# Turning q, k and x on TensorE in halves of 64 tokens instead of by DMA, and starting the row pairs two head pairs earlier

## The chip, the cores and the metric

The kernel runs on one core of one Trainium2 chip. The metric is the device time of one execution in microseconds. Three runs of the kernel before gave 306.70, 307.38 and 309.17 us, median 307.38. TensorE is called PE here, VectorE DVE, ScalarE ACT, GpSimd POOL, and SyncE SP.

## What is computed

Attention with a relative bias that depends on the distance of two tokens alone, and behind it a network of three gates, of which the largest counts:

```python
batch, n_heads, seq, head_dim = (8, 8, 576, 64)
...
scores = scale * np.matmul(q, k.transpose(0, 1, 3, 2))
...
scores = scores + bias.transpose(2, 0, 1)[None, :, :, :]
...
attn = np.exp(scores)
attn = attn / (np.sum(attn, axis=-1, keepdims=True) + 1e-09)
return np.matmul(attn, v).astype(np.float32)
...
h = np.maximum(np.maximum(x @ w1, x @ w2), x @ w3)
return (h @ w_out).astype(np.float32)
```

Inputs and output are float32. x is the attention's output as 4608 tokens of 512, the gates are 512 x 768, and `w_out` is 768 x 512.

## The kernel before

**Tiles.** The work is ordered by batch index (8) and, within it, by pair of heads (4): 32 pairs. Two heads of 64 fill the 128 partitions of `qT` and `kT`, which hold q and k with the head's dimension on the partitions and the tokens along the row. The 576 tokens are four tiles of 128 and a tail of 64. The tail's keys of both heads lie in one tile (`ktail`), head 0 in rows 0 to 63 and head 1 in rows 64 to 127.

**One pair.** PE makes the scores with keys on the partitions (`scores`, or `key_scores` where 512 queries of one key tile are made at once), ACT writes their exponentials to `e`, DVE multiplies the band near the diagonal by the exponentials of the bias (`times_band`). The tail's keys and queries go the same way (`left_keys`, `left_queries`, tile `el`). In the next pair PE multiplies `e` and `el` by the values and a column of ones (`attend`, `attend_rows`, tile `a`), and DVE divides by the sums and writes `x_sb` (`quotients`). The network needs x with the 512 features on the partitions, `xT`.

**The network beside it.** Its products are spread over the pairs in portions of 512 tokens. `ffn` makes a portion. From (2, 2) on, that is from batch index 2, pair 2, three pairs take two blocks of gates each and a fourth pair takes the outputs. What is left over waits in a list `pending`, out of which `fill` takes products.

**Row pairs.** From `ROWS = (3, 0)` on, every matmul works on 64 rows, two at a time on the two halves of the array, each with a PSUM bank of its own. `pair` (line 364) issues one half of such a product's matmuls, then with the halves swapped the other. In such a pair `run` of `gates` or of `outputs` fixes the order: first 8 matmuls of the first product, the third gate's largest value of the pair before on DVE, the fourth score tile, bands, the other 8 matmuls, ACT's copy, the second product, between them the left queries and the next pair's first score tile. The two pools for sums and for the network hold one tile of two banks each there, in place of two of one bank.

**PSUM.** All score tiles, `sc`, `sct` and `scq`, and the tiles `tp` in which q and k of batch index 1 are turned, take turns in the two buffers of one pool (`ps_s`, two banks a buffer). A tile that is given a buffer waits for the last reader of the tile before the last.

**Turning.** Batch index 0 is turned on PE (`first_transposes`, `more_transposes`, `x_transposes`). So is q and k of batch index 1 (`second_transposes`, line 781): ten transposes of 128 x 128 for a pair, q into one bank and k into the other, and two copies by DVE and two by ACT, declared independent as they read different banks. For batch indices 2 to 7 q and k are turned by DMA: `transposes` (line 724) puts 10 transposes for a batch index on SP's queue, and `turn_ahead` places them one batch index ahead. x of batch indices 1 to 7 is turned by DMA as well, five transposes for a batch index, from `quotients` of its last pair (lines 973 and 1021). SP also carries the early loads and the stores of the output.

**Loads.** POOL issues the loads. `begin_qk` loads half of a batch index's q and k two batch indices ahead; the rest and v follow one ahead. `in_turn` holds a load back until the loads some places before it have landed.

**Order.** PE, DVE and most of ACT keep the order of the program (`inorder`). From batch index 2, pair 2, on that holds for all exponentials; before, the exponentials may be moved by the scheduler.

Of the kernel before, what the change touches and what calls it, by code (L numbers as in the profile page):

```python
# [39 lines left out]
def kernel(  # L40
# [12 lines left out]
    nc = tc.nc  # L53
# [3 lines left out]
    P = 128  # L57
# [3 lines left out]
    QS = 2 * P  # L61
    QM = 2 * QS
    KT = 4
    ROWS = (3, 0)
    DEEP = 6
    PACKETS = 6 * QM
    FCH = d_ff // P
# [32 lines left out]
    def free_banks():  # L100
        ps_f.release()
        ps_a.release()
# [9 lines left out]
    def tr(*args):  # L112
        inorder(nc.tensor.transpose(*args))
# [14 lines left out]
    def other_banks(later, earlier):  # L128

        for a in later:  # L130
            for b in earlier:
                tc.declare_no_dep(a.ins, b.ins, reason="they read different PSUM banks")
# [588 lines left out]
            hook()  # L721


    def transposes(b):

        made = qk_tiles()
        qk.append(made)

        def pair(g):
            for j in range(2):  # L730
                inorder(nc.sync.dma_start_transpose(  # L731
                    out=made[j][:, g, 0 : KT * P].rearrange("p (t n) -> p t n", t=KT),
                    in_=batch[b][j][:, g].rearrange("p t h d -> p (t h d)"),
                ))

        def left():
            for j, n in enumerate((S - KT * P, P)):
                inorder(nc.sync.dma_start_transpose(  # L738
                    out=made[j][:, :, KT * P : KT * P + n],
                    in_=(qtail, ktail)[j][b % 2][0:n].rearrange("p h c -> p (h c)"),  # L740
                ))

        return [lambda: pair(0), left] + [lambda g=g: pair(g) for g in range(1, HP)]

    def qk_tiles():
        return [qkt.tile([P, HP, n], BF16, tag=x, name=x) for x, n in (("qT", S), ("kT", (KT + 1) * P))]

# [30 lines left out]
        tr(tp[:, QS : QS + P], qtail[0][:, hp, :], ident[:])  # L778
        dve_copy(qk[0][0][:, hp, QS:], tp[:, 0 : S - QS])

    def second_transposes(made, hp):

        hs = slice(2 * hp, 2 * hp + 2)
        tp = ps_s.tile([P, 2, 2 * CH], BF16, tag="sc", name="tp")
        for j, tl in enumerate((qtail, ktail)):
            for t in range(KT):
                tr(tp[:, j, P * t : P * t + P], batch[1][j][:, t, hs, :].rearrange("p h d -> p (h d)"), ident[:])
            tr(tp[:, j, KT * P : KT * P + P], tl[1][:, hp, :], ident[:])
        main = [
            copy(  # L790
                made[j][:, hp, 0 : KT * P].rearrange("c (p t) -> c p t", t=KT),
                tp[:, j, 0 : KT * P].rearrange("c (t p) -> c p t", t=KT),
            )
            for j, copy in enumerate((dve_copy, act_copy))
        ]
        tail = [
            copy(made[j][:, hp, KT * P :], tp[:, j, KT * P : n])
            for j, (copy, n) in enumerate(((dve_copy, S), (act_copy, (KT + 1) * P)))
        ]
        other_banks([main[1], tail[1]], [main[0], tail[0]])  # L800
        other_banks([tail[0]], [main[1]])

    def times_band(hp, e4, t, lo, hi, put=lambda x: x):
        lo, hi = max(lo, P * t - P), min(hi, P * t + 2 * P)
# [121 lines left out]
    def attend(b, hp, e4, el, half):  # L926

        x = ps_a.tile([P, 6, AW], F32, tag="a", name="a")
        v, vl = vx[b % 2], vt[b % 2]
        for i in range(2):
            t = 2 * half + i
            c = slice(P * t, P * t + P)
            mm(
                x[:, 2 * i : 2 * i + 2, :], lhsT=el[:, c], rhs=vl[:, hp, :, 0:AW],
                start=True, stop=False, skip_group_check=True,
            )
            for par in range(2):  # L940
                for kt in range(KT):
                    mm(
                        x[:, 2 * i + par, :], lhsT=e4[:, kt, par, c], rhs=v[:, kt, 2 * hp + par, 0:AW],
                        start=False, stop=(kt == KT - 1), skip_group_check=True,
                    )
        n = 2 + half
        if half:
            mm(
                x[:, 4:6, :], lhsT=el[:, S - P : S], rhs=vl[:, hp, :, 0:AW],
                start=True, stop=False, skip_group_check=True,  # L950
            )
            for par in range(2):
                for kt in range(KT):
                    mm(
                        x[:, 4 + par, :], lhsT=el[:, S - 64 + P * kt + 64 * par :][:, 0:P],
                        rhs=v[:, kt, 2 * hp + par, 0:AW],
                        start=False, stop=(kt == KT - 1), skip_group_check=True,
                    )

        def quotients():  # L960
            rd = nrm.tile([P, 6], F32, tag="rd", name="rd")
            inorder(nc.vector.reciprocal(rd[:, 0 : 2 * n], x[:, 0 : 2 * n, D]))
            divided[b, hp, half] = inorder(nc.vector.tensor_tensor(
                out=x_sb[b][:, 2 * half : 2 * half + n, P * hp : P * hp + P].rearrange("p t (h d) -> p t h d", d=D),
                in0=x[:, 0 : 2 * n, 0:D].rearrange("p (t h) d -> p t h d", h=2),
                in1=rd[:, 0 : 2 * n].rearrange("p (t h) -> p t h", h=2).unsqueeze(3).to_broadcast([P, n, 2, D]),
                op=ALU.mult,
            ))
            if b and hp == HP - 1:
                for t in range(2 * half, 2 * half + 2 + half):  # L970
                    c = b * S + P * t
                    w = min(P, S - P * t)
                    inorder(nc.sync.dma_start_transpose(out=xT[:, :, c : c + w], in_=x_sb[b][P - w :, t, :]))
        return quotients

    def attend_rows(b, hp, e4, el):
# [28 lines left out]
        def end():  # L1005
            behind_rows(rows(True)[0], last)

            def quotients():
                n = KT + 1
                rd = nrm.tile([P, 2, n], F32, tag="rd", name="rd")  # L1010
                a = x[:, :, 0 : n * AW].rearrange("p h (t d) -> p h t d", d=AW)
                inorder(nc.vector.reciprocal(rd[:], a[:, :, :, D]))
                inorder(nc.vector.tensor_tensor(
                    out=x_sb[b][:, 0:n, P * hp : P * hp + P].rearrange("p t (h d) -> p h t d", d=D),
                    in0=a[:, :, :, 0:D], in1=rd[:].unsqueeze(3).to_broadcast([P, 2, n, D]), op=ALU.mult,
                ))
                if hp == HP - 1:
                    for t in range(n):
                        c = b * S + P * t
                        w = min(P, S - P * t)  # L1020
                        inorder(nc.sync.dma_start_transpose(out=xT[:, :, c : c + w], in_=x_sb[b][P - w :, t, :]))
            return quotients
        return end

# [107 lines left out]
    for hp in range(HP):  # L1132
# [42 lines left out]
        else:  # L1175
# [11 lines left out]
            if hp == 2:  # L1187
                x_transposes(2, 0)
                x_transposes(3, 0)
            else:  # L1190
                begin_qk(2)
                x_transposes(0, 1)
                fill(8, lambda: second_transposes(qk[1], 0))
            products(hp, el)
        late.append(lambda hp=hp, e4=e4, el=el: attend(0, hp, e4, el, 1))

    turns = {n: [] for n in range(2, B)}
    places = {2: ((1, 1, 0), (1, 1, 1), (1, 2, 0), (1, 3, 1), (2, 1, 0)), 3: ((2, 2, 0), (2, 2, 1), (2, 3, 0), (3, 0, 0), (3, 0, 1))}
    for n in range(4, B):
        places[n] = tuple((n - 1, hp, half) for hp, half in ((1, 0), (1, 1), (2, 0), (2, 1), (3, 0)))  # L1200

    def turn_ahead(*place):

        for n, order in places.items():
            if place == order[0]:
                turns[n] = transposes(n)
            if place in order:
                turns[n].pop(0)()

    turned = [lambda hp=hp: x_transposes(hp, 1) for hp in range(1, HP)]  # L1210
    for b, hp in [(b, hp) for b in range(1, B) for hp in range(HP)]:
# [5 lines left out]
        tiled = bool(stages)  # L1217
        rows = (b, hp) >= ROWS
        if (b, hp) == ROWS:
            free_banks()  # L1220
            ps_a, ps_f = banks(1)
            pending.clear()
            thirds = [after]
        rate = 8 if b == 1 or (b, hp) == (2, 0) else 13


# [13 lines left out]
            for c, tt in order[:2]:  # L1240
                scores(qT, kT, e4, c, tt)
        store_outputs()
        turn_ahead(b, hp, 0)
        early()
        if turned:
            turned.pop(0)()
# [19 lines left out]
        if rows:  # L1266
# [19 lines left out]
            def ahead():  # L1286
# [3 lines left out]
                    key_scores(*(x[:, n % HP, :] for x in qk[n // HP]), begun[0][0], 0)  # L1290

            run(
                lambda: key_scores(qT, kT, e4, 3), left, ahead, largest, bands, lambda: left_keys_rows(qT, kT, el)
            )
            thirds.append(after)
        elif tiled:
# [35 lines left out]

            visit(qT, kT, e4, order[2:], None if together else beside_scores, el=el if together else None)
        store_outputs()
        turn_ahead(b, hp, 1)
        early()
        if turned:
            turned.pop(0)()
        if not together:
            quotients = next_late()  # L1340
            times_band(hp, e4, 1, 0, QM, inorder)
            quotients()
        if b == 1 and hp + 1 < HP:
            second_transposes(qk[1], hp + 1)
        if hp == 1 and b > 1:
            pending.extend((n, [fn]) for n, fn in rest)
            rest.clear()
# [1 line left out]
        if hp == 1 and b + 1 < B:  # L1349
# [81 lines left out]
```

## Time and profile before

| | |
|---|---|
| the runs' median | 307.38 us (306.70 to 309.17) |
| the profiled execution's own time | 306.96 us |
| its span, first to last instruction | 305.2 us |
| granted TensorE clock | 1.00 |
| PE busy from 72.05 to 96.63 us, pairs (2, 2) to (3, 0) | 23.99 of 24.58 us |
| PE busy from 96.63 to 245.85 us, pairs (3, 1) to (7, 3) | 148.96 of 149.22 us |
| PE busy from 245.85 us to the end | 55.58 of 59.35 us |
| transposes by DMA on SP's queue | 95 |

The span counts from the first to the last instruction of the program; the execution's own time has some 1.8 us more. A pair begins where PE starts on the sums of the pair before, `a<-vt,el`. Those starts are at 183.22, 191.01, 199.36 and 206.73 us: a pair with gates takes 7.79 us, the one with outputs 8.35, and the one behind it 7.37, since there a shorter product stands in the third gate's place. Matmuls overlap in the rows of the time line: a duration shown is that of the whole way through the array, and the work of a matmul is better read from the distance between two starts.

### The profile page before, as it was taken

The numbers are of one execution on the slowest core, as the hardware profiler recorded it, in microseconds if no ns is written. First come the engines' busy times: TensorE is split into PE (matmuls) and PEld (weight loads), VectorE is DVE, ScalarE is ACT, GpSimd is POOL, SyncE is SP. The second block draws the span as 40 slices with busy tenths as digits, with TensorE's granted clock in tenths as the row PEclk, the third lists the DMA queues.
The fourth block names the chain that finished last, engine by engine and source line by source line (L and its number), as shares of the span: only waits on it lengthen the run. The fifth ranks groups of instructions, "written<-read, shape, count | busy, mean of one in ns | idle before, by whom it ended". The sixth has DMA issues, their size and how long they took to land.

```text
span 305.2 us, 11001 instructions
## 1 busy us (share of the span) xinstructions
PE 295.5 (97%) x4745; PEld 183.7 (60%) x4745; DVE 206.3 (68%) x455; ACT 201.3 (66%) x270; POOL 143.7 (47%) x199
## 2 busy tenths in 40 slices
PE   8789999999999999999999999999999999999995
PEld 2367877765656676567666766676667654444442
DVE  6489888777776677676777677767776765453552
ACT  3999988977786787768776877677777720222211
POOL 8989677725839746774676469462000000000000
PEclk9999999999999999999999999999999999999999
DMA  9999999999999999999999999999623013202003
GB/s 160 187 203 194 176 137 120 114 165 128 223 150 121 150 131 205 174 143 192 181 139 135 202 162 146 138 197 171 79 46 140 6 40 94 84 0 108 31 0 137
DMA packets 165776, 40.51 MB, mean 133 GB/s; under 512 B 154584, under 2 KB 161248, under 8 KB 165728
## 3 DMA queue, kind: packets, MB, share of 16 engines
q0 software_dynamic: 105664, 16.66, 95.5%
q1 hardware_dynamic: 58304, 22.69, 41.6%
q8 instruction: 37, 0.61, 0.8%
q10 hardware_dynamic: 1760, 0.47, 0.7%
q14 instruction: 11, 0.09, 0.1%
HBM read 35.39 MB, written 9.45 MB: 147 GB/s over the span
## 4 chain that ended last, share of the span: by engine, by line
PE 80%; ACT 7%; DMA 6%; DVE 3%; SPq 2%; issue 1%; DVEq 0%; ACTq 0%
PE psp L109 32%; PE ps L109 15%; PE a L109 12%; PE sc L109 8%; PE pso L109 6%; ACT e L827 5%; DMA kT<-ktail 5%; PE sct L109 2%; PE warm L109 1%; PE scq L109 1%; ACT el L827 1%; SPq L738 1%; SPq L731 1%; DVE e L807 1%; DMA out_dram<-osb 1%
## 5 line engine op out<-in xcount | busy, mean ns | idle before, releaser
L827 ACT ACTIVATE e<-sc 128x1024 bf16<-128x1024 f32 x128 | 129.0, 1026 | 29.3 <-PE sc L109 28.0
L109 PEld LDWEIGHTS <-w_bf 64*128 64x128 bf16 (+1 forms) x1112 | 75.8, 95 | 55.3 <-issue 1.9
L109 PE MATMUL psp<-xT,w_bf 64*128 64x512 bf16 x784 | 97.2, 376 | 0.0
L807 DVE TENSOR_TENSOR e<-e,hank 128x512 bf16<-128x512 bf16 (+2 forms) x120 | 56.1, 473 | 13.9 <-ACT e L827 13.2
L109 PE MATMUL ps<-xT,w_bf 128*128 128x512 bf16 (+1 forms) x328 | 59.1, 332 | 0.0
L109 PE MATMUL sc<-qT,kT 64*128 64x256 bf16 (+1 forms) x352 | 48.5, 319 | 2.3 <-ACT e L827 1.1
L109 PEld LDWEIGHTS <-kT 64*128 64x128 bf16 (+1 forms) x712 | 30.0, 94 | 24.8 <-issue 6.8
L109 PE MATMUL a<-vx,e 64*128 64x65 bf16 (+1 forms) x1664 | 44.9, 190 | 0.0
L199 POOL DMA_DIRECT2D k_sb<-in_k_dram x48 | 36.2, 764 | 17.8 <-DMA vx<-in_v_dram 7.8
L199 POOL DMA_DIRECT2D q_sb<-in_q_dram x48 | 36.4, 767 | 15.1 <-DMA vx<-in_v_dram 5.7
L109 PEld LDWEIGHTS <-e 64*128 64x128 bf16 (+1 forms) x1664 | 40.8, 95 | 4.3
L109 PEld LDWEIGHTS <-hT 64*128 64x128 bf16 (+1 forms) x462 | 28.3, 95 | 18.7 <-DVE hT L551 1.6
L167 POOL DMA_DIRECT2D vx<-in_v_dram x28 | 24.8, 893 | 19.5 <-PE a L109 5.4
L109 PE MATMUL psp<-wo_bf,hT 64*128 64x256 bf16 (+1 forms) x360 | 31.7, 305 | 0.0
L421 ACT ACTIVATE m<-ps 128x512 bf16<-128x512 f32 x14 | 8.4, 597 | 34.3 <-PE ps L109 34.3
L827 ACT ACTIVATE el<-sct 128x576 bf16<-128x576 f32 (+2 forms) x36 | 21.7, 605 | 14.0 <-PE sct L109 13.9
L109 PEld LDWEIGHTS <-el 64*128 64x128 bf16 (+1 forms) x676 | 26.4, 94 | 7.0 <-issue 4.4
L109 PE MATMUL a<-vt,el 64*128 64x65 bf16 (+1 forms) x260 | 29.5, 198 | 0.2 <-DVE m L511 0.2
L551 DVE TENSOR_TENSOR hT<-psp,m 128x1024 bf16<-128x1024 f32 (+1 forms) x20 | 18.7, 956 | 9.1 <-PE psp L109 9.1
L109 PE MATMUL pso<-wo_bf,hT 128*128 128x512 bf16 (+2 forms) x102 | 21.7, 366 | 0.0
L430 DVE TENSOR_TENSOR m<-ps,m 128x512 bf16<-128x512 f32 x14 | 9.7, 692 | 17.0 <-PE ps L109 17.0
L537 DVE TENSOR_TENSOR m<-psp,m 128x1024 bf16<-128x1024 f32 x15 | 18.4, 1225 | 3.3 <-PE psp L109 3.1
(82 smaller groups left out, 292.8 us busy)
## 6 DMA issues: line engine op xcount, KB each, us to landing
out_dram<-osb SPq DMA_DIRECT2D x35, 256.0 KB, 4.7
vx<-in_v_dram POOLq DMA_DIRECT2D x28, 128.0 KB, 6.7
q_sb<-in_q_dram POOLq DMA_DIRECT2D x50, 64.0 KB, 5.3
k_sb<-in_k_dram POOLq DMA_DIRECT2D x48, 64.0 KB, 5.3
w_bf<-in_moe_w_dram POOLq DMA_DIRECT2D x2, 512.0 KB, 8.5
xT<-in_k_dram SPq DMA_DIRECT2D x6, 128.0 KB, 4.5
hank<-w_dr SPq DMA_DIRECT2D x2, 384.0 KB, 5.7
w_bf<-in_moe_w_dram POOLq DMA_DIRECT2D x1, 768.0 KB, 8.1
```

Source lines behind the costliest of these rows:

```text
L109: made = inorder(nc.tensor.matmul(*args, **kw))
L167: in_turn(b, nc.gpsimd.dma_start(out=dst[:, t, h0:h1, :], in_=x[:, t, h0:h1, :]), P * (h1 - h0))
L199: in_turn(b, nc.gpsimd.dma_start(out=dst[:, g, :, par, :], in_=part), KT * P)
L421: nc.scalar.activation(out=st[fb]["m0"][:], in_=ps0, func=ACTF.Copy)
L430: inorder(nc.vector.tensor_tensor(out=m[:], in0=ps1, in1=st[fb]["m0"][:], op=ALU.max))
L537: return lambda: inorder(nc.vector.tensor_tensor(out=m[0][:], in0=ps1(), in1=m[0][:], op=ALU.max,))
L551: inorder(nc.vector.tensor_tensor(out=out_[:, i : i + n], in0=ps2()[:, i : i + n], in1=m[0][:, i : i + n], op=ALU.max,))
L731: inorder(nc.sync.dma_start_transpose(out=made[j][:, g, 0 : KT * P].rearrange("p (t n) -> p t n", t=KT), in_=batch[b][j][:, g].rearrange(" ...
L738: inorder(nc.sync.dma_start_transpose(out=made[j][:, :, KT * P : KT * P + n], in_=(qtail, ktail)[j][b % 2][0:n].rearrange("p h c -> p (h c)"),
L807: put(nc.vector.tensor_tensor(out=e4[:, t, :, lo:hi], in0=e4[:, t, :, lo:hi], in1=hank[:, 2 * hp : 2 * hp + 2, c0:c1][:, :, ::-1], op=ALU. ...
L827: made = nc.scalar.activation(out=out_, in_=in_, func=ACTF.Exp, scale=inv_sqrt_d)
```

## The change

The transposes by DMA are gone, and with them `transposes`, `second_transposes` and the order by places. A function `turn(n)` is called once in each pair n (32 pairs, n = 4 b + hp), from pair 3 on and once behind the last. It turns on PE q and k of pair n + 1 and x of pair n - 1 (q and k up to batch index 7, x from batch index 1), each block of 128 tokens as two halves: 64 tokens on 64 rows, whose transpose of 128 x 64 goes to one bank of `tp` for the upper half and to the other for the lower. Tails are single halves or, for k, one pair. All lie in one tile of the pool of the scores. Every copy out of `tp` takes both halves, so it reads both banks: DVE copies q, q's tail and x, ACT copies k and x's tail. The declarations of independence are gone. A copy of batch index 1's q and k scatters the tokens, as before; from batch index 2 on the runs are 64 long.

Where it stands: in a row pair ahead of the fourth score tile, inside `run`; before the row pairs at the end of the pair, ahead of the last products and of the next pair's scores. Row pairs begin at (2, 2), and what is pending is drained ahead of them. `begin_qk` follows pair 2, not 1.

```diff
-    ROWS = (3, 0)
+    ROWS = (2, 2)
...
-    def second_transposes(made, hp):
+    def turn(n):
         tp = ps_s.tile([P, 2, 2 * CH], BF16, tag="sc", name="tp")
+        W = KT * 64
+        K, X = W + 64, 2 * W + 128
+        def half(h, c, src):
+            r = slice(64 * h, 64 * h + 64)
+            tr(tp[:, h, c : c + 64], src[r], ident[r, r])
+        def halves(c, src):
+            for h in range(2):
+                half(h, c, src)
...
+        b, hp = divmod(n + 1, HP)
+        new = b < B
+        if new:
...
+            for j, c in enumerate((0, K)):
+                for t in range(KT):
+                    part = batch[b][j][:, hp, t] if b > 1 else batch[b][j][:, t, 2 * hp : 2 * hp + 2]
+                    halves(c + 64 * t, part.rearrange("p h d -> p (h d)"))
+            halves(K + W, ktail[b % 2][:, hp, :])
+            half(0, W, qtail[b % 2][:, hp, :])
...
+        b_x, hp_x = divmod(n - 1, HP)
+        if b_x:
+            x = x_sb[b_x][:, :, P * hp_x : P * hp_x + P]
+            half(1, X + W, x[:, KT])
             for t in range(KT):
+                halves(X + 64 * t, x[:, t])
+        if new:
+            if b > 1:
+                dve_copy(by_half(q_to[:, 0 : KT * P], KT), turned(0, KT))
+                act_copy(by_half(k_to, KT + 1), turned(K, KT + 1))
+            else:
...
+            dve_copy(q_to[:, KT * P : S], tp[:, 0, W : W + 64])
+        if b_x:
+            to = xT[:, hp_x, b_x * S : b_x * S + S]
+            dve_copy(by_half(to[:, 0 : KT * P], KT), turned(X, KT))
+            act_copy(to[:, KT * P :], tp[:, 1, X + W : X + W + 64])
...
-        other_banks([main[1], tail[1]], [main[0], tail[0]])
-        other_banks([tail[0]], [main[1]])
...
         if (b, hp) == ROWS:
+            while pending:
+                fill(13)
             free_banks()
             ps_a, ps_f = banks(1)
             pending.clear()
-            thirds = [after]
+            thirds = [lambda: (lambda: None, lambda parts=1: lambda: None)]
...
-        turn_ahead(b, hp, 0)
...
             run(
-                lambda: key_scores(qT, kT, e4, 3), left, ahead, largest, bands, lambda: left_keys_rows(qT, kT, el)
+                lambda: (turn(HP * b + hp), key_scores(qT, kT, e4, 3)), left, ahead, largest, bands,
+                lambda: left_keys_rows(qT, kT, el),
             )
...
-        turn_ahead(b, hp, 1)
...
-        if b == 1 and hp + 1 < HP:
-            second_transposes(qk[1], hp + 1)
+        if not rows:
+            turn(HP * b + hp)
...
-        if hp == (2 if b == 1 else 1) and b + 2 < B:
+        if hp == 2 and b + 2 < B:
             begin_qk(b + 2)
...
     for put in [next_late() for _ in late[:]]:
         put()
+    turn(HP * B)
     fill(13)
```

More of the change, by code (lines that the diff above doesn't have):

```diff
@@ L721, in fill @@
             hook()
[L724 to L743, printed above, removed]
     def qk_tiles():
@@ L779, in more_transposes, with by_half, turned @@
         dve_copy(qk[0][0][:, hp, QS:], tp[:, 0 : S - QS])
-    def second_transposes(made, hp):
-        hs = slice(2 * hp, 2 * hp + 2)
+    def turn(n):
         tp = ps_s.tile([P, 2, 2 * CH], BF16, tag="sc", name="tp")
-        for j, tl in enumerate((qtail, ktail)):
-            for t in range(KT):
[L787 to L799, printed above, removed]
-        other_banks([main[1], tail[1]], [main[0], tail[0]])
-        other_banks([tail[0]], [main[1]])
+        W = KT * 64
[6 more added lines that the diff above has]
+                half(h, c, src)
+        def by_half(x, n):
+            return x.rearrange("c (t h n) -> c t h n", h=2, t=n)
+        def turned(c, n):
+            return tp[:, :, c : c + 64 * n].rearrange("c h (t n) -> c t h n", t=n)
+        b, hp = divmod(n + 1, HP)
+        new = b < B
+        if new:
+            if len(qk) == b:
+                qk.append(qk_tiles())
+            for j, c in enumerate((0, K)):
[4 more added lines that the diff above has]
+            half(0, W, qtail[b % 2][:, hp, :])
+            q_to, k_to = (x[:, hp, :] for x in qk[b])
+        b_x, hp_x = divmod(n - 1, HP)
+        if b_x:
+            x = x_sb[b_x][:, :, P * hp_x : P * hp_x + P]
+            half(1, X + W, x[:, KT])
+            for t in range(KT):
+                halves(X + 64 * t, x[:, t])
[4 more added lines that the diff above has]
+            else:
+                for copy, to, c in ((dve_copy, q_to, 0), (act_copy, k_to, K)):
+                    copy(to[:, 0 : KT * P].rearrange("c (h n t) -> c t h n", h=2, t=KT), turned(c, KT))
+                act_copy(by_half(k_to[:, KT * P :], 1), turned(K + W, 1))
+            dve_copy(q_to[:, KT * P : S], tp[:, 0, W : W + 64])
[3 more added lines that the diff above has]
+            act_copy(to[:, KT * P :], tp[:, 1, X + W : X + W + 64])
@@ L968, in quotients @@
             ))
[L969 to L973, printed above, removed]
         return quotients
@@ L1016, in quotients @@
                 ))
[L1017 to L1021, printed above, removed]
             return quotients
@@ L1192 @@
                 x_transposes(0, 1)
-                fill(8, lambda: second_transposes(qk[1], 0))
+                fill(8, lambda: turn(HP - 1))
             products(hp, el)
         late.append(lambda hp=hp, e4=e4, el=el: attend(0, hp, e4, el, 1))
[L1197 to L1208, printed above, removed]
     turned = [lambda hp=hp: x_transposes(hp, 1) for hp in range(1, HP)]
```

## The prediction, made before the result was known

> **What bounds the kernel now.** I read the page first, then the time line of one pair of heads in the middle, then the groups with their shapes kept apart, then the waits and the chain. A "pair" is one turn of the main loop, one pair of heads of one batch index; (3, 0) is batch index 3, pair 0.
>
> ```profile
> PE 295.5 (97%) x4745; PEld 183.7 (60%) x4745; DVE 206.3 (68%) x455; ACT 201.3 (66%) x270; POOL 143.7 (47%) x199
> ...
> PE 80%; ACT 7%; DMA 6%; DVE 3%; SPq 2%; issue 1%; DVEq 0%; ACTq 0%
> ```
>
> TensorE is the bound. The time line of pair (6, 0), from the first `a<-vt,el` at 183.22 to the next at 191.01, shows it without a hole (7.79 us; "PE psp x16" are two blocks of 0.86):
>
> ```profile
> 187.21 1.23 DVE L551 TENSOR_TENSOR hT<-psp,m 128x1024 bf16<-128x1024 f32 x1 [0.60 <-PE psp L109]
> ...
> 187.86 0.39 PE L109 MATMUL sc<-qT,kT 64*128 64x512 bf16 x2
> ...
> 188.09 1.90 PE L109 MATMUL psp<-xT,w_bf 64*128 64x512 bf16 x16
> 188.29 1.03 ACT L827 ACTIVATE e<-sc 128x1024 bf16<-128x1024 f32 x1 [0.53 <-PE sc L109]
> ...
> 189.21 1.02 ACT L123 ACTIVATE m<-psp 128x1024 bf16<-128x1024 f32 x1
> ...
> 189.81 0.30 PE L109 MATMUL scq<-qT,kT 64*128 64x64 bf16 x8
> 189.93 0.40 PE L109 MATMUL sc<-qT,kT 64*128 64x512 bf16 x2
> ...
> 190.15 1.04 PE L109 MATMUL psp<-xT,w_bf 64*128 64x512 bf16 x8
> ...
> 191.01 0.21 PE L109 MATMUL a<-vt,el 64*128 64x65 bf16 x2
> ```
>
> The new copies are priced from these groups:
>
> ```profile
> L827 ACT ACTIVATE e<-sc 128x1024 bf16<-128x1024 f32 x128 | 129.0, 1026 | 29.3 <-PE sc L109 28.0 <-issue 1.0
> ...
> L126 DVE COPY qT<-tp 128x512 bf16<-128x512 bf16 x4 | 2.7, 684 | 0.5 <-PE tp L113 0.5
> L123 ACT ACTIVATE kT<-tp 128x512 bf16<-128x512 bf16 x4 | 2.5, 624 | 0.0
> ...
> L123 ACT ACTIVATE kT<-tp 128x128 bf16<-128x128 bf16 x4 | 1.2, 312 | 0.0
> ...
> L126 DVE COPY kT<-tp 128x640 bf16<-128x640 bf16 x2 | 1.0, 481 | 0.0
> ...
> L126 DVE COPY kT<-tp 128x512 bf16<-128x512 bf16 x2 | 0.8, 420 | 0.0
> ...
> L126 DVE COPY qT<-tp 128x64 bf16<-128x64 bf16 x4 | 0.7, 181 | 0.0
> ```
>
> What the DMA transposes cost today is in the chain and in the waits:
>
> ```profile
> 82.17 8.31 DMA kT<-ktail
> ```
> ```profile
> PEld L109 <- DMA kT<-ktail: 0.8, 2, 0.5
> ```
>
> The chain gives one wait 8.31 us, but PE was busy for all of it but the last half microsecond. The waits say 0.8 us; the gaps between matmul starts are 0.51 us at 90.53 and 0.42 at 122.18. That is all there is to win: 0.9 us.
>
> **What goes.** 95 transposes leave SP's queue (q 24, k 24, tails 12, x 35); SP keeps loads and stores. Worth 0.9 us. Rows from (2, 2): in a row pair the sums' five tail products of 130 columns become pairs of 65 (0.13 us), and the left keys' 576 columns pairs of 288 (0.12). 0.25 us twice is 0.5; it is inside the pair times below. POOL's eleven loads of `begin_qk` go one pair later; their first reader is then five pairs (40 us) off and they land in about 5.3 us, so nothing. If that cover were gone, a late load would cost up to those 5.3 us.
>
> **What PE gets.** 28 turns of 19 halves (q, k) and 28 of 9 (x), 784 matmuls of 64 columns. Eight such ones, `scq`, take 0.12 us (189.81 to 189.93), 15 ns each: 12.1 us. Forty whole transposes at 56 ns go: net 9.8 us. In a pair: 0.43 us.
>
> **What stands behind it.** In a row pair the turn stands after the first 8 `psp` matmuls of the gate, ahead of the fourth score tile. Its tile `tp` takes one of the two buffers in which all score tiles go round. I read the waits of the built changed program: the copies out of `tp` wait for one another, since each reads both banks. DVE q (512), then ACT k (640), then DVE q tail (64), DVE x (512), then ACT x (64). Behind ACT's last one stand, in its queue, the exponentials of the fourth score tile, the gate's copy, the left queries and the next pair's first scores. PE's `scq` waits for the last copy (same buffer), PE's next `sc` for the exponentials of the fourth tile.
>
> Prices: q 0.42, as the 512-element copy in unbroken runs (the 684 ns one scatters its output; that is the upper bound); k by ACT's two rows, 312 + (640-128)/384 x 312 = 728 ns; q tail 0.18; x 0.42; x's rest 0.26 (same line). A hand-over between engines is 0.035 us in this trace, PE to a reader about 0.2 after the last issue. Chain: 0.42+0.73+0.18+0.42+0.26 and four hand-overs = 2.14 us.
>
> The Trainium skill, "PSUM — Partial Sum Buffer", section "PSUM bank collisions raise a hardware error", says two engines must not read one bank at once, so such readers are ordered. The old `second_transposes` kept its engines to one bank each, and the trace has them side by side:
>
> ```profile
> 44.20 0.78 DVE L126 COPY qT<-tp 128x512 bf16<-128x512 bf16 x2
> 44.27 0.80 ACT L123 ACTIVATE kT<-tp 128x512 bf16<-128x512 bf16 x2
> ```
>
> By that row alone the copies would take 1.05 us, by the rule 2.14; the waits of the program decide for 2.14.
>
> **A gate pair, step by step** (0 is its first `a<-vt,el`). PE reaches the turn at 4.64 today. Once the pair before ends late, 0.12 is added at the sums (they wait for `el<-el,hank`) and 0.2 at the third gate (its bank is freed by DVE's `m`): 4.95. Then the turn 0.43 and 0.2 to DVE: 5.58 (DVE's `hT` is done at 5.52). Copies: 7.72. Exponentials: 8.75. Next `sc` at 8.79, 0.22, last 8 `psp` 0.86: the pair ends at 9.87, and the next begins in the same state. Against 7.79: +2.08. Meanwhile PE has only 2.06 us (`sc` 0.22, `psp` 0.86 twice, `scq` 0.12) to hide 3.4.
>
> An output pair (8.35 today, (6, 1)): turn at 5.08, copies done at 7.87, and PE, which has 0.65 us to do after the turn, waits 1.75 for `scq`; then 2.9 us of its outputs and the scores, end 10.9. The pair after it (7.37 today): turn at 4.21, then 0.63 to DVE's start, 2.14 of copies, 1.07 of exponentials and hand-over, 1.08 of scores and `psp`: 9.15.
>
> Sum from 72.05 to 245.85 (173.8 us today): (2, 2) 10.7 (1.3 of waiting outputs, drained ahead of it; then, with no third gate of a pair before, the turn at 4.5, + 4.92 as above), (2, 3) and (3, 0) 9.87 each; five output pairs 54.5; five after them 45.75; eight gate pairs 79.0; (7, 3), which turns x alone, 8.1. Together 217.8: +44.0.
>
> **Before the rows** seven turns stand ahead of the next pair's scores. Those wait for k; the second score tile takes `tp`'s buffer and, with x in the turn, ACT puts the exponentials of the first tile ahead of x's rest. At 43.30: `x_sb` is done at 44.29, q (scattered) 44.97, k 45.95 (0.62 and, for its tail, 0.31), q tail 46.16, x 46.61, exponentials 47.1, x's rest 47.4: the second tile at 47.4, not 45.9, less 0.1 on PE: 1.4. At 50.50 less work covers it: 2.2. The turns ahead of (2, 0) and (2, 1), new ones with 0.87 us of cover: 2.5 each. The first two have no x: 0.9 and 0.35. The last has 2.6 us of outputs as cover: 0.5. Sum 10.4; bounds 5 (PE alone and half the waits) and 14 (every turn 2).
>
> **At the end** PE waits for the last `x_sb` (248.42, where it goes on at 247.35 today), then 9 halves: 1.2 us.
>
> Sum against the profiled execution's own 306.96 (span 305.2; 0.42 under the median of the three runs): 306.96 + 44.0 + 10.4 + 1.2 = 362.6. The median may lie 0.4 off that; I say 362. PE's 9.8 us are in it.
>
> Bounds: without the 0.3 in each pair and with 5 ahead of the rows, 306.96 + 38 + 5 + 1 = 351; with q and x at 684 ns, 0.52 in each of 21 turns, 373. Own range of this case: 350 to 375.
>
> **Rivals.**
> *Not slower: the DMA wait was real.* If the 8.31 and the 6.87 us that the chain gives `kT<-ktail` held PE, 15.2 go and 9.8 come, with the copies hidden: 301.6. It decides from 9.8 us of true waiting on; the gaps show 0.9. Chance 0.02.
> *PE's own work alone.* Copies hidden: 306.96 + 9.8 + 1.2 - 0.9 - 0.5 = 316.6. For it: ACT is busy 66%, DVE 68%. Against: the buffer is wanted 2.06 us after the turn. 0.04.
> *The copies run side by side* (1.05 in place of 2.14): 21 x 1.09 and 5 ahead of the rows less: 335. Against: the waits in the program. 0.07.
> *Copies at the slow rate, or the halves not two abreast* (0.43 more each): 373 to 375. For it: no row has runs of 64 that hop between two banks. 0.13.
> *The forecast:* 0.74.
>
> **How the numbers follow.** Time 362, of the likeliest. The range leaves out the first three rivals (0.13) and the edges: 344 to 377. One per cent is about what a measurement of this kernel can tell from none. Faster 0.02 (the first rival), within 1% 0.01, slower 0.97.
>
> **What would show it.** Gate pairs of 9.9 us, output pairs of 10.9; in each, ACT's `kT<-tp` right behind DVE's `qT<-tp` and DVE's tail copy behind that; PE waiting for ACT `xT` ahead of `scq` and for ACT `e` ahead of `sc`; PE's share down from 97% to about 86%; 64-column transposes at 15 ns. It is wrong if `scq` and `sc` start without a wait, if the q copy is not 0.42, or if the first turns cost nothing.

## The result and the profile after

The kernel after takes 364.69 us (median of 4 runs, 362.63 to 366.80), the kernel before 307.04 (4 runs, 306.62 to 309.17): a ratio of 1.186, 95% interval 1.177 to 1.195. The profiled execution took 362.63 us, its span is 360.9. The page of the kernel after has, against the lines shown of before:

```profile
PE 316.8 (88%) x5567; PEld 197.9 (55%) x5575; DVE 228.9 (63%) x524; ACT 223.9 (62%) x320; POOL 143.3 (40%) x199
...
PE 66%; ACT 18%; DVE 12%; issue 2%; DMA 1%; ACTq 0%
PE psp L109 22%; PE ps L109 13%; PE a L109 11%; ACT e L836 9%; PE sc L109 7%; ACT kT L123 6%; DVE qT L126 5%; PE pso L109 5%; PE tp L113 3%; DVE xT L126 2%; PE sct L109 2%; ACT xT L123 1%; PE warm L109 1%; DVE x_sb L972 1%; ACT el L836 1%
```

PE's share falls from 97% to 88%, though it is busy 21 us longer. The chain was on PE for 80% and is for 66%; ACT and DVE come in with the copies `kT`, `qT`, `xT` and with the exponentials `e` behind them.

The waits of the kernel after (us in total, times, longest) name the same links:

```profile
ACT kT L123 <- DVE qT L126: 30.2, 28, 1.8
DVE qT L126 <- ACT kT L123: 24.4, 28, 1.5
ACT xT L123 <- DVE xT L126: 18.1, 25, 3.5
...
PE sc L109 <- ACT e L836: 14.8, 23, 1.2
...
PE scq L109 <- ACT xT L123: 7.2, 6, 1.4
```

The time line of a gate pair of the kernel after, from its first `a<-vt,el` at 225.57 us to the next at 234.86, shows where the time goes. It answers to the pair from 183.22 to 191.01 of before.

```profile
230.22 0.30 PE L113 MATMUL tp<-ident,q_sb 64*128 64x64 bf16 x8
...
230.62 0.40 PE L109 MATMUL sc<-qT,kT 64*128 64x512 bf16 x2
...
230.84 0.42 DVE L126 COPY qT<-tp 128x512 bf16<-128x512 bf16 x1
231.30 0.70 ACT L123 ACTIVATE kT<-tp 128x640 bf16<-128x640 bf16 x1 [1.19 <-DVE qT L126]
...
232.04 0.19 DVE L126 COPY qT<-tp 128x64 bf16<-128x64 bf16 x1 [0.77 <-ACT kT L123]
232.15 0.41 DVE L126 COPY xT<-tp 128x512 bf16<-128x512 bf16 x1
...
232.59 0.22 ACT L123 ACTIVATE xT<-tp 128x64 bf16<-128x64 bf16 x1 [0.59 <-DVE xT L126]
232.71 1.02 ACT L836 ACTIVATE e<-sc 128x1024 bf16<-128x1024 f32 x1
232.87 0.29 PE L109 MATMUL scq<-qT,kT 64*128 64x64 bf16 x8
...
233.78 0.39 PE L109 MATMUL sc<-qT,kT 64*128 64x512 bf16 x2 [0.62 <-ACT e L836]
```

Read it downward: the bracket of a copy names the copy ahead of it, on the other engine. The fourth score tile is done at 231.02, but ACT, which must make its exponentials, stands in the row of copies until 232.71. Of these 1.69 us ACT spends 0.82 on its own two copies and waits 0.87 for DVE's. Counted by starts, PE loses time twice. Its 16 products from 230.84 on are issued by 232.56 (0.86 us for 8), but `scq` starts at 232.87, 0.06 us behind the last copy. And the next `sc` starts 0.91 us after `scq`, where it took 0.12 in the kernel before, because it waits for the exponentials. These 0.3 and 0.8 us are all that the pair takes beyond PE's own pace, which e1 below puts at 8.18 us. In an output pair PE has less to do meanwhile and stands longer, for the last copy. The time line of PE in the one from 234.86 to 245.33 us has:

```profile
242.32 0.29 PE L109 MATMUL scq<-qT,kT 64*128 64x64 bf16 x8 [1.42 <-ACT xT L123]
```

**Where the 55.7 us of span are.** The span splits at the first sums of (2, 2) and at the last pair's `a<-vt,el` (93.71 and 300.04 us after; 72.05 and 245.85 before):

| stretch | before | after | more | predicted |
|---|---|---|---|---|
| ahead of the rows | 72.05 | 93.71 | 21.7 | 11.7 (10.4 and 1.3 of drain) |
| row pairs | 173.8 | 206.3 | 32.5 | 42.7 (44.0 less that drain) |
| end | 59.35 | 60.86 | 1.5 | 1.2 |

The sum came out (55.6 predicted) because two errors of about 10 us cancel; that is luck. The experiments must explain both, not only the total.

### The profile page after: what moved, and what is told of

Read it like the earlier page. It is cut to its first block, busy times and chain, and to the rows that moved or that the text cites. A ratio compares the mean times of both kernels' runs of the same rounds, so it can differ in the third digit from the quotient of the medians.

```text
span 360.9 us, 12575 instructions
## 1 busy us (share of the span) xinstructions
PE 316.8 (88%) x5567; PEld 197.9 (55%) x5575; DVE 228.9 (63%) x524; ACT 223.9 (62%) x320; POOL 143.3 (40%) x199
## 4 chain that ended last, share of the span: by engine, by line
PE 66%; ACT 18%; DVE 12%; issue 2%; DMA 1%; ACTq 0%
PE psp L109 22%; PE ps L109 13%; PE a L109 11%; ACT e L836 9%; PE sc L109 7%; ACT kT L123 6%; DVE qT L126 5%; PE pso L109 5%; PE tp L113 3%; DVE xT L126 2%; PE sct L109 2%; ACT xT L123 1%; PE warm L109 1%; DVE x_sb L972 1%; ACT el L836 1%
## 5 line engine op out<-in xcount | busy, mean ns | idle before, releaser
L109 PE MATMUL psp<-xT,w_bf 64*128 64x512 bf16 x800 | 99.2, 376 | 0.6 <-DVE x_sb L1017 0.6
L109 PE MATMUL sc<-qT,kT 64*128 64x512 bf16 (+1 forms) x336 | 49.7, 329 | 22.2 <-ACT e L836 14.8
L816 DVE TENSOR_TENSOR e<-e,hank 128x512 bf16<-128x512 bf16 (+2 forms) x120 | 56.1, 472 | 14.6 <-ACT e L836 14.4
L109 PEld LDWEIGHTS <-kT 64*128 64x128 bf16 (+1 forms) x700 | 30.5, 94 | 57.1 <-issue 37.4
L126 DVE COPY qT<-tp 128x512 bf16<-128x512 bf16 (+3 forms) x63 | 22.9, 363 | 38.3 <-ACT kT L123 24.4
L109 PE MATMUL a<-vx,e 64*128 64x65 bf16 (+1 forms) x1728 | 45.7, 191 | 0.0
L109 PEld LDWEIGHTS <-e 64*128 64x128 bf16 (+1 forms) x1728 | 41.6, 95 | 4.2
L123 ACT ACTIVATE kT<-tp 128x640 bf16<-128x640 bf16 (+2 forms) x32 | 22.5, 735 | 30.2 <-DVE qT L126 30.2
L109 PEld LDWEIGHTS <-hT 64*128 64x128 bf16 (+1 forms) x462 | 29.5, 95 | 16.0 <-DVE hT L436 0.4
L109 PEld LDWEIGHTS <-el 64*128 64x128 bf16 (+1 forms) x702 | 27.5, 95 | 6.1 <-issue 3.5
L551 DVE TENSOR_TENSOR hT<-psp,m 128x1024 bf16<-128x1024 f32 (+1 forms) x21 | 19.9, 968 | 8.2 <-PE psp L109 8.2
```

What stands on the lines that cost most here:

```text
L109: made = inorder(nc.tensor.matmul(*args, **kw))
L123: return inorder(nc.scalar.activation(out=out_, in_=in_, func=ACTF.Copy))
L126: return inorder(nc.vector.tensor_copy(out_, in_))
L551: inorder(nc.vector.tensor_tensor(out=out_[:, i : i + n], in0=ps2()[:, i : i + n], in1=m[0][:, i : i + n], op=ALU.max,))
L816: put(nc.vector.tensor_tensor(out=e4[:, t, :, lo:hi], in0=e4[:, t, :, lo:hi], in1=hank[:, 2 * hp : 2 * hp + 2, c0:c1][:, :, ::-1], op=ALU. ...
```

## The experiments

The theory is that of the prediction: the copies out of `tp` hand over between DVE and ACT one after the other, ACT's queue stands behind them, and PE waits for what stands in that queue. Its rivals: PE's own transposes cost the time; the amount of copying costs it, whoever copies; the row pairs from (2, 2) on cost it. Ratios are to runs of the kernel before on the same chip, with 95% intervals. It took 306.8 to 307.7 us (medians) on these chips and 307.04 beside the kernel after, so differences in us to the kernel after may be off by some 1 us.

**e1, the transposes alone.** The kernel before, with the halves turned on PE as in the kernel after, from batch index 2 on for q and k, and nobody reading them; the DMA transposes stay.

```diff
+    def turn(n):      # as in the kernel after, the matmuls alone
...
-                lambda: key_scores(qT, kT, e4, 3), left, ahead, largest, bands, lambda: left_keys_rows(qT, kT, el)
+                lambda: (turn(HP * b + hp), key_scores(qT, kT, e4, 3)), left, ahead, largest, bands,
+                lambda: left_keys_rows(qT, kT, el),
...
+        if not rows and HP * b + hp > HP:
+            turn(HP * b + hp)
...
-        if hp == (2 if b == 1 else 1) and b + 2 < B:
+        if hp == 2 and b + 2 < B:
...
+    turn(HP * B)
```

> The kernel before, with the new 64-row transposes added where the changed kernel has them (q and k from batch index 2 on, x), but into a tile that nobody copies: the DMA transposes still do the work, and the transposes' own result is not used. This leaves PE's part of the change alone. Theory A (the copies out of tp, which wait for one another, make the row pairs long): 714 halves at 15 ns are 11 us, and ahead of the rows x waits for x_sb about 1 us at each of four turns and once at the end, so 316 to 324 us, gate pairs of 8.2 us. Theory B (PE's extra work and the two-buffer pool as such are the cost): at least half of the 57 us, so over 335 us, gate pairs over 8.8.

Measured: 326.97 us, ratio 1.062 (1.057 to 1.068), above the expected 316 to 324 and under the 335 of theory B. In the steady pairs it is what 28 halves at 14 to 15 ns make: gate pairs of 8.18 to 8.20 us (7.79 before), output pairs 8.75 (8.35), the pairs behind them 7.77 (7.37), so 0.4 each. That makes 8 us in 20 pairs. The whole is 19 us because there are halves ahead of the rows too, because the turns there and at the end wait for the division and for exponentials (4.7 us in six waits), and because of single standstills. The largest is in PE's time line of this kernel:

```profile
120.83 0.28 PE L109 MATMUL a<-vx,el 64*128 64x65 bf16 x6
123.15 0.20 PE L109 MATMUL a<-vx,el 64*128 64x65 bf16 x2 [2.05 <-issue]
...
123.32 1.42 PE L109 MATMUL psp<-xT,w_bf 64*128 64x512 bf16 x8
```

PE stands for 2.05 us amid eight like matmuls, for nothing that the profile shows, and the eight `psp` behind it take 1.42 us where they take 1.04 elsewhere. All that PE does itself, these waits and standstills with it, is about a third of the loss of 57.65 us. It isn't the bulk.

**e2 and e9, the row pairs from (2, 2) on, alone.** The kernel before with that part of the change; e9 is the same program once more, for a second trace.

```diff
-    ROWS = (3, 0)
+    ROWS = (2, 2)
...
+            while pending:
+                fill(13)
...
-            thirds = [after]
+            thirds = [lambda: (lambda: None, lambda parts=1: lambda: None)]
```

> The kernel before with ROWS = (2, 2) and the drain ahead of it, all else as it was, DMA transposes included. From the sums: 0.25 us less in each of two pairs, 306.0 to 307.3 us. Rival: the drain and the start of the rows at (2, 2), without a third gate to fill it, cost more than the pairs save, 308 to 310 us.

> The same kernel as with ROWS = (2, 2) alone, looked at once more. There PE stood still for 0.6 to 1.5 us at four places in the row pairs with no waiting that the profile shows. If those places belong to the program (its order, its addresses), they come back at the same matmuls, and the span is 309 to 311 us. If they are chance (a late fetch of code or of data), they lie elsewhere or are fewer, and the span is anywhere from 305.5 to 311.

Measured: e2 312.02 us (311.75 over the five runs that the ratio uses), ratio 1.013 (1.008 to 1.018), above both expectations; e9 309.98 in a single run. The prediction had put 0.5 us of gain here. It is a small loss. In both traces the pair (2, 2) begins later than in the kernel before (73.08 us in e9 against 72.05), and PE waits twice at the start of the rows, where there is no third gate to fill in. Both also have standstills in the middle of the rows. PE's time line of e9, at the start of the rows:

```profile
74.19 0.39 PE L109 MATMUL sc<-qT,kT 64*128 64x512 bf16 x2 [0.20 <-ACT e L827]
...
76.36 1.04 PE L109 MATMUL psp<-xT,w_bf 64*128 64x512 bf16 x8 [0.60 <-DVE x_sb L1013]
```

A standstill in the middle of the rows, in the same view of e9:

```profile
179.98 0.24 PE L109 MATMUL a<-vx,el 64*128 64x65 bf16 x4 [1.07 <-issue]
```

The same one in PE's time line of e2:

```profile
181.73 0.24 PE L109 MATMUL a<-vx,el 64*128 64x65 bf16 x4 [1.06 <-issue]
```

Three standstills lie ahead of the same matmuls in both traces: `psp` in (3, 0), 0.77 us in e2 and 1.14 in e9; `psp` in (4, 3), 1.36 and 0.20; and the one shown, in (5, 3). Another of 0.44 us is in e2 alone, and one of 0.77 in e9 alone. So most of the places come with the program, though the lengths do not. Together they are 3.6 us in e2 and 3.2 in e9, and the spans are 4.7 and 3.0 us longer than before: they are most of the loss, or all of it. The drain makes (2, 2) begin 1.0 us later in e9, but (2, 2) and (2, 3) are 1.1 us shorter together in e2 (15.1 against 16.2), both waits included. Why PE stands with no wait in the profile is open. The kernel after starts its rows at (2, 2) as well and has no such standstill, so this loss can't be counted as a part of its own.

**e3, the same copies, all on DVE.** The kernel after, with ACT's copies out of `tp` given to DVE.

```diff
-                act_copy(by_half(k_to, KT + 1), turned(K, KT + 1))
+                dve_copy(by_half(k_to, KT + 1), turned(K, KT + 1))
...
-                for copy, to, c in ((dve_copy, q_to, 0), (act_copy, k_to, K)):
+                for copy, to, c in ((dve_copy, q_to, 0), (dve_copy, k_to, K)):
...
-                act_copy(by_half(k_to[:, KT * P :], 1), turned(K + W, 1))
+                dve_copy(by_half(k_to[:, KT * P :], 1), turned(K + W, 1))
...
-            act_copy(to[:, KT * P :], tp[:, 1, X + W : X + W + 64])
+            dve_copy(to[:, KT * P :], tp[:, 1, X + W : X + W + 64])
```

> The changed kernel with all copies out of tp on DVE, so no copy waits for another engine and none stands in ACT's queue; the amount of copying is the same, and DVE gets about 0.8 us more in each pair. Theory A (the hand-overs and ACT's queue behind them): the hold falls from 2.0 to about 1.55 us and the fourth tile's exponentials no longer wait, so scq and sc find their buffers free: gate pairs 8.2 to 8.4 (9.29 now), output pairs 8.8 (10.46), 336 to 342 us in all. Theory B (the amount of copying on engines that are two thirds busy): DVE has more to do, so gate pairs stay at 9.3 or grow, 364 to 375 us.

Measured: 334.17 us, ratio 1.086 (1.081 to 1.092), 30.5 us less than the kernel after and somewhat under the expected 336 to 342. In the traces 22.0 us of it are in the row pairs. All of the copies are still made, one after the other, and DVE is busier (243.7 us, 74%). What is gone is the handing over, and ACT's own two copies. The time line of a gate pair of e3:

```profile
208.63 0.40 PE L109 MATMUL sc<-qT,kT 64*128 64x512 bf16 x2
...
208.85 0.42 DVE L126 COPY qT<-tp 128x512 bf16<-128x512 bf16 x1
...
209.06 1.02 ACT L836 ACTIVATE e<-sc 128x1024 bf16<-128x1024 f32 x1 [0.94 <-PE sc L109]
209.19 0.48 DVE L126 COPY kT<-tp 128x640 bf16<-128x640 bf16 x1
209.58 0.18 DVE L126 COPY qT<-tp 128x64 bf16<-128x64 bf16 x1
...
209.68 0.51 DVE L126 COPY xT<-tp 128x512 bf16<-128x512 bf16 x2
...
210.57 0.29 PE L109 MATMUL scq<-qT,kT 64*128 64x64 bf16 x8
...
210.69 0.40 PE L109 MATMUL sc<-qT,kT 64*128 64x512 bf16 x2
```

ACT begins the exponentials at once, 0.43 us after `sc` starts, where it took 2.09 in the kernel after, and PE's `scq` and `sc` stand without a wait. Gate pairs take 8.18 to 8.20 us, which is e1's pace, that of PE. So the amount of copying isn't the cause. It is that copies stand in ACT's queue ahead of the exponentials, each waiting for one of DVE's. No run keeps ACT's copies and takes away their waits, so the shares of the two (0.82 and 0.87 us in the pair above) are read from one row and not tested. Output pairs still take 9.60 (8.75 in e1, 8.8 expected): there `scq` comes too soon behind the turn. PE's time line of e3 has in one of them:

```profile
218.36 0.29 PE L109 MATMUL scq<-qT,kT 64*128 64x64 bf16 x8 [0.68 <-ACT e L836]
```

The profile puts this wait down to ACT's exponentials, which end at 218.30. In the kernel after, though, `scq` starts at 242.32 while they still run, so it is rather the copies that hold the buffer: x's of 512 elements ends at 218.32.

**e5, the turn behind the fourth score tile.** The kernel after, with the two swapped, so that ACT has the exponentials to make while DVE copies q.

```diff
-                lambda: (turn(HP * b + hp), key_scores(qT, kT, e4, 3)), left, ahead, largest, bands,
+                lambda: (key_scores(qT, kT, e4, 3), turn(HP * b + hp)), left, ahead, largest, bands,
```

> The changed kernel with the turn of a row pair one step later, behind the fourth score tile: the same work, the same waits from copy to copy, but the copies no longer stand ahead of that tile's exponentials in ACT's queue. The left queries then take the fourth tile's buffer, and the next pair's first scores take tp's. Theory A (the copies cost by what stands behind them): exponentials done at about 6.1 us of the pair, in place of 8.2, copies done at about 7.5, so the scores wait about 0.5 us in place of 0.9: gate pairs 8.6 to 8.9 (9.29 now), output pairs about 9.1 (10.46), 346 to 354 us. Rival (what counts is how long tp is held): the wait moves from the left queries to the scores, gate pairs within 0.2 of 9.29, 361 to 366 us.

Measured: 347.24 us, ratio 1.130 (1.120 to 1.139), 17 us less than after. Gate pairs 8.64, output pairs 9.32, the pairs behind them 8.20. The time line of a gate pair of e5:

```profile
221.32 1.02 ACT L836 ACTIVATE e<-sc 128x1024 bf16<-128x1024 f32 x1 [0.53 <-PE sc L109]
...
223.80 0.39 PE L109 MATMUL sc<-qT,kT 64*128 64x512 bf16 x2 [0.27 <-ACT xT L123]
```

The chain of copies is untouched, only one set of exponentials stands ahead of it in ACT's queue. So ACT's place in that queue, and not the copies' duration, was worth more than half of what a gate pair lost beyond PE's pace (0.65 of 1.11 us). What is left is the next `sc`, which now takes `tp`'s buffer and waits for the last copy out of it: the length of the chain costs something too.

**e6, x by DMA again, q and k on PE.** The kernel after, with x's part of `turn` gone and x's DMA transposes back in both `quotients`.

```diff
+        if n + 1 >= HP * B:
+            return
...
-        b_x, hp_x = divmod(n - 1, HP)
+        b_x, hp_x = 0, 0
...
+                    inorder(nc.sync.dma_start_transpose(out=xT[:, :, c : c + w], in_=x_sb[b][P - w :, t, :]))
```

> The changed kernel with x turned by DMA as before, q and k on PE. The chain of copies loses its last two links (x on DVE, x's rest on ACT), and PE loses 9 halves a turn. Theory A: in a gate pair the exponentials of the fourth tile start behind the k copy, at 6.3 us of the pair instead of 7.1, gate pairs 8.4 to 8.6 (9.29), output pairs 9.3 to 9.6 (10.46); ahead of the rows the wait for x_sb goes, 4 us: 336 to 344 us in all. Rival (q and k are the cost, x rides along): 355 us or more.

Measured: 335.21 us, ratio 1.090 (1.083 to 1.098), 29.5 us less than after, just under the expected 336 to 344. Gate pairs 8.34, output pairs 9.74, the pairs behind them 7.92. The time line of a gate pair of e6:

```profile
205.06 0.42 DVE L126 COPY qT<-tp 128x512 bf16<-128x512 bf16 x1
...
205.51 0.70 ACT L123 ACTIVATE kT<-tp 128x640 bf16<-128x640 bf16 x1 [1.05 <-DVE qT L126]
...
206.12 1.02 ACT L838 ACTIVATE e<-sc 128x1024 bf16<-128x1024 f32 x1
...
206.79 0.29 PE L109 MATMUL scq<-qT,kT 64*128 64x64 bf16 x8
...
207.18 0.39 PE L109 MATMUL sc<-qT,kT 64*128 64x512 bf16 x2
```

With x out of it ACT's one copy, k, comes second in the chain, and the exponentials begin right behind it, 1.06 us after DVE's q copy starts in place of 1.87. So x's two copies at the end of the chain, the second of them on ACT, make most of what the chain is longer than its cover, but not all: `sc` still starts 0.39 us after `scq`, behind the exponentials, where 0.12 would do.

**e4, unbroken writes for batch index 1.** The kernel after, with each main copy of batch index 1 in two parts, one for each bank, that write without gaps and read with a stride.

```diff
-                    copy(to[:, 0 : KT * P].rearrange("c (h n t) -> c t h n", h=2, t=KT), turned(c, KT))
+                    for h in range(2):
+                        copy(
+                            to[:, 256 * h : 256 * h + 256].rearrange("c (n t) -> c n t", t=KT),
+                            tp[:, h, c : c + 256].rearrange("c (t n) -> c n t", n=64),
+                        )
```

> The changed kernel, with batch index 1's main copies of q and k written unbroken (the PSUM side is read with a stride), in two parts each; they took 1.30 us each, where the old ones, written unbroken, took 0.68 and 0.62. If the scattered writes are what lengthens the first turns, each of four turns gets about 1 us shorter: 360 to 362 us. Rival: those copies lie beside other work, 364 to 365 us.

Measured: 359.38 us, ratio 1.165 (1.159 to 1.172), 5.3 us less than after, just under the expected 360 to 362. The group of the kernel after, shapes kept apart (busy us, mean ns):

```profile
L123 ACT ACTIVATE kT<-tp 128x512 bf16<-128x512 bf16 x4 | 5.2, 1301 | 5.5 <-DVE qT L126 5.5
```

In e4 the copies have become these two rows, q's with three copies of batch index 0 in it; the third line, from the time line, is both parts of one q:

```profile
L126 DVE COPY qT<-tp 128x256 bf16<-128x256 bf16 x11 | 3.9, 383 | 4.3 <-PE tp L113 4.3
L123 ACT ACTIVATE kT<-tp 128x256 bf16<-128x256 bf16 x8 | 2.6, 381 | 3.4 <-DVE qT L126 3.4
...
45.75 0.76 DVE L126 COPY qT<-tp 128x256 bf16<-128x256 bf16 x2 [0.41 <-PE tp L113]
```

1.30 us for 512 elements that are written eight bytes apart, 0.76 for the same in two unbroken parts. What it did to a turn stands in the time line of the kernel after, at the end of (1, 1):

```profile
58.52 0.56 DVE L972 TENSOR_TENSOR x_sb<-a,rd 128x384 bf16<-128x384 f32 x1
...
59.14 0.32 PE L113 MATMUL tp<-ident,x_sb 64*128 64x64 bf16 x9 [0.83 <-DVE x_sb L972]
...
59.49 1.30 DVE L126 COPY qT<-tp 128x512 bf16<-128x512 bf16 x1 [0.41 <-PE tp L113]
60.82 1.40 ACT L123 ACTIVATE kT<-tp 128x512 bf16<-128x512 bf16 x2 [1.71 <-DVE qT L126]
...
62.18 0.39 PE L109 MATMUL sc<-qT,kT 64*128 64x256 bf16 x4 [1.75 <-ACT kT L123]
```

2.7 us pass between q's start and the first scores, with 1.05 us of products as PE's cover; and PE has stood 0.83 us before, for the division.

**e8, x one pair later.** The kernel after, with x of pair n - 2 turned in pair n, so that its division is long done.

```diff
-        b_x, hp_x = divmod(n - 1, HP)
+        b_x, hp_x = divmod(n - 2, HP)
...
+    turn(HP * B + 1)
```

> The changed kernel with x turned one pair later and nothing else. If PE's wait for x_sb ahead of the rows (0.9 us or so at each of five turns) and at the end (1 us) is a cost of its own: 358 to 361 us. Rival: the copies are what the next scores wait for there anyway, so nothing is gained: 363 to 366 us.

Measured: 360.71 us, ratio 1.174 (1.167 to 1.180), 4.0 us less than after; the two ratios' intervals just touch (1.177 to 1.195 after), so the size is rough. Row pairs are as in the kernel after, so the gain lies ahead of the rows and at the end: 1.7 and 1.0 us in the two traces.

**e7 and e10, the cures together.** e7 is the kernel after with the edits of e3, e4 and e8; e10 adds that of e5.

```diff
+                dve_copy(by_half(k_to, KT + 1), turned(K, KT + 1))
...
+                    for h in range(2):
...
+        b_x, hp_x = divmod(n - 2, HP)
...
+                lambda: (key_scores(qT, kT, e4, 3), turn(HP * b + hp)), left, ahead, largest, bands,
```

> Three repairs together: all copies on DVE, batch index 1's copies written unbroken, and x turned one pair later (x of pair n - 2 in turn n, so its transposes no longer wait for the division just ahead of them; the last of them behind the first products at the end). From 334.2 us with DVE alone: about 4 us less for the unbroken copies and 4 to 5 for x, 324 to 328 us. It stays slower than the kernel before, since PE's own 10 us remain. If the repairs hide one another: 330 us or more.

> The three repairs together with the turn behind the fourth score tile. Gate pairs already run at PE's pace (8.18 us, 7.79 and 0.4 for the transposes) and should stay there; output pairs (9.6) still wait for tp at the left queries, which now take the fourth tile's buffer instead: about 9.1 us, so 323 to 325 us in all. If the output pairs' 0.8 us above PE's pace have another cause, they stay at 9.6 and the time at 326.

Measured: e7 325.99 us, ratio 1.060 (1.055 to 1.066); e10 325.30, ratio 1.056 (1.048 to 1.065). The two can't be told apart: once ACT makes no copies there is little left for e5's edit to free, except in the output pairs (9.60 in e7, 9.19 in e10). Both are some 39 us faster than the kernel after, and both are slower than the kernel before. In e10's span of 324.5 us the rows take 182.3 us, 8.5 more than before: about 0.4 us in each steady pair and another 0.4 in each of the five output pairs, while (2, 2) to (3, 0) are 0.5 us shorter together. The stretch ahead of the rows ends at 82.41, 10.4 later (79.53 in e7, 7.5 later). PE's time line of e10 has there, among others:

```profile
24.07 0.30 PE L113 MATMUL xp<-ident,x_sb 128*128 128x128 bf16 x2 [1.93 <-DVE qT L126]
...
77.45 0.29 PE L113 MATMUL tp<-ident,q_sb 64*128 64x64 bf16 x8 [1.22 <-ACT e L840]
```

All such waits of at least 0.15 us between 23 and 82 us add up to 5.3 us, against 0.3 before. The first of them lies ahead of the first turn, which PE reaches at 33.35 us in e10 and at 30.64 in e7, and e7 does not have it; so it isn't the change's. The others, 3.4 us, are waits for copies on DVE and for exponentials, at turns that still have little work as cover (in e7 all are 3.7 us). The rest isn't resolved.

## Why the prediction was right, and where it was not

The total (362 us predicted, 364.69 measured), the sign and the mechanism were right, the division of the total was not. That the total came so close is luck: 10 us too much for the rows and 10 us too little for what is ahead of them.

- *What there was to win (0.9 us).* Right. The steady pairs are 8.18 to 8.20 us in e1, which keeps the DMA transposes, and in e3, which has none. The chain's 8.31 us for `kT<-ktail` were no wait of PE's. The loads land in 3.0 to 3.3 us now, where the prediction counted 5.3, and nothing seen here came of it.
- *PE's transposes (15 ns a half, 0.43 us a pair).* Right: 0.40 in each steady pair of e1. The rival "PE's own work alone" at 316.6 fell even for e1, at 326.97: it left out the waits for the division and for exponentials, and the standstills without a cause in the profile.
- *The order of the copies.* Right in every link: q on DVE, k on ACT, q's tail and x on DVE, x's rest on ACT, then the exponentials, then `sc`. The Trainium skill, "PSUM — Partial Sum Buffer", section "PSUM bank collisions raise a hardware error", has readers of one bank kept apart, and here ACT's k copy starts 0.04 us behind the end of DVE's q copy. The rival with copies side by side (335) fell in this order; e3 reached 334.17 by another way, with the copies still in a row.
- *The length of that chain (2.14 us).* Too long: from q's start to the exponentials' it is 1.87 (230.84 to 232.71). The single prices held (q 0.42, k 0.70, tail 0.19, x 0.41, x's rest 0.22), but neighbours on one engine overlap: x's copy starts 0.11 us after a tail copy of 0.19 has started.
- *A gate pair of 9.87 us.* It takes 9.29. The step that failed is "0.12 is added at the sums" and "0.2 at the third gate: 4.95". The turn is reached 4.65 us into the pair, as before the change, so these waits did not come. With the 0.27 of the chain that is the whole difference. Output pairs take 10.46 (10.9 predicted), the pairs behind them 8.86 (9.15). Over 20 pairs this makes the 10 us by which the rows were overestimated.
- *Ahead of the rows 10.4.* PE's waits of at least 0.15 us from 23 us on add up to 14.4 us there in the kernel after. The step that failed is "q (scattered) 44.97, k 45.95 (0.62 and, for its tail, 0.31)". The prediction takes the 684 ns copy for one that scatters its output, and the section on the change says that batch index 1 is scattered "as before". In the kernel before these copies read with a stride and write without gaps, while those of after write with a stride: 1.30 us each for q and k. So 684 ns was no upper bound. e4 gives 5.3 us for it. Second, x's wait for the division was put on DVE's start alone, while PE's nine halves stand in its queue for it, and all products behind them: e8 gives 4.0 us, the end's share included. Third, the granted clock fell behind two of the standstills, about 3.3 us by estimate (a mean clock of 0.991 over 360.9 us), which nothing in the trace of before could show. Fourth, the last turn ahead of the rows waits 1.22 us for ACT's exponentials before its first transpose (at 88.75 us; e1 has the same wait at 74.07), and the prediction has 0.5 for that whole turn. These sizes overlap, as the traces of e4 and e8 lose more to the clock than that of the kernel after, and are no exact sum; together they are of the size of the missing 10 us.
- *"Rows from (2, 2) ... 0.5 us" of gain.* Wrong in sign: e2 loses 1.3% (0.8% to 1.8%). Most of that is standstills of unknown cause, which the kernel after doesn't have, so what the earlier rows are worth in it isn't shown.
- *Slow copies or halves not two abreast (373 to 375).* Fell in the rows, where q takes 0.42. For batch index 1 it was worse than this rival's price.

## What to carry to other kernels

If several copies out of one PSUM tile each touch both its banks, as here, splitting them over two engines may not share the work; here it made a chain that also held up the second engine's queue. Try giving the whole row to the engine whose queue is not the next thing that PE waits for (30.5 us here), or putting the other engine's urgent work ahead of its copy (17 us). A third way, one bank for each engine as in the kernel before, wasn't tried for these halves. A price from the trace of before belongs to a shape with its strides on both sides: look at which side is broken before you use it.

## What the runs showed of the hardware

**The granted clock falls behind a standstill of less than 2 us.** The windows of the kernel after (us, then PE, PEld, DVE, ACT, POOL busy, then PE's clock, DMA share, GB/s):

```profile
31.60:33.40 1.80, 0.04 (x3) 0.01 (x2) 0.40 (x1) 1.37 (x2) 1.29 (x3) 1.00 1.81 179
33.40:36.80 3.40, 3.40 (x41) 2.50 (x42) 1.84 (x7) 2.31 (x4) 1.77 (x4) 0.55 2.31 161
...
73.20:74.40 1.20, 0.04 (x2) 0.04 (x3) 1.20 (x4) 1.11 (x2) 0.00 (x0) 1.00 0.00 0
74.40:78.00 3.60, 3.60 (x56) 2.71 (x55) 1.81 (x6) 2.37 (x5) 0.00 (x0) 1.00 0.02 5
```

And those of e1, around its standstill:

```profile
121.00:123.10 2.10, 0.10 (x7) 0.00 (x0) 0.14 (x1) 0.57 (x1) 0.96 (x3) 1.00 1.37 78
123.10:127.00 3.90, 3.85 (x26) 1.57 (x28) 1.51 (x3) 1.56 (x2) 2.39 (x4) 0.59 1.82 213
```

After 1.8 us of standstill the clock is 0.55 for 3.4 us, after 2.1 us 0.59 for 3.9; after 1.2 us it stays at 1.00 here, and so it does after 1.36 us in e2 (149.96). But in e4 it is 0.58 behind a standstill of 1.17 us (66.50 to 67.67), and the kernel after has its second fall behind one of 1.18 us (63.75), 0.4 us of work after one of 1.75. In windows of half a microsecond its clock is 0.50 from 34.0 to 37.0 and from 64.5 to 67.5 us, and 1.00 again from 37.5 and from 68.0 on. By estimate such a stretch costs a further 1.5 us or so (3.4 us at 0.55). The Trainium skill, "TensorE: Matmul & The Clock Gate", section "What's actually happening", gives at least one idle window of about 3.4 us as the condition of a fall, and about 3.4 us of steady work until the clock is back. The way back agrees; the fall came after much shorter standstills. What decides whether it comes wasn't tried.

**Strided writes.** 512 two-byte elements a row out of PSUM, written eight bytes apart: 1.30 us on DVE and on ACT alike. Written without gaps and read with a stride they took 0.68 and 0.62 (kernel before), or in two parts 0.76 together on DVE and 0.38 each on ACT (e4).

**Standstills that the profile can't place.** PE stood 2.05 us in e1, 1.06 and 1.07 in e2 and e9, each amid like matmuls and with "issue" as the label. In e2 and e9 three fall on the same matmuls, two of them with different lengths, and each trace has one of its own. No other trace kept here has one of 0.15 us or more after its first 25 us. e1, e2 and e9 are the kernels of the experiments that still turn q and k by DMA, but the kernel before does too and has none. No run isolates their cause.
